# One slot earlier for the second part of batch 0 and the projections of batch 1, in a fused attention and GLU kernel

## The chip, the cores and the metric

The kernel runs on one core of one Trainium2 chip. The metric is the device time of that core in microseconds, as a median over runs. Beside the times there is one profiled execution, whose instructions are told by engine: PE is TensorE (PEld its weight loads), DVE is VectorE, ACT is ScalarE, POOL is GpSimd, SP is SyncE, which issues most of the transfers.

## The reference, cut to what matters

```
# q, k, v: (4 batches, 4 heads, 1088 tokens, 32) float32; S1, S2: (8, 32); x @ w in 128 -> 1536
phi(x) = outer(S1 x, S2 x).reshape(64)            # per token and head
kv, z  = sum_s phi(k_s) v_s^T, sum_s phi(k_s)     # per batch and head
attn   = phi(q) kv / (phi(q) z + 1e-6)
x      = attn transposed to (4352 tokens, 128)
out    = (sigmoid(x @ w_gate) * (x @ w_val)) @ w_out      # d_ff = 1536
```

S1, S2 and the three weight matrices arrive as 64-bit floats. The kernel reads them as pairs of 32-bit words and turns them into 32-bit floats itself.

## The kernel before, in words

The second half, the gated layer, is cut into chunks of 512 tokens (`tok_chk`: eight of 512 and one of 256). A chunk takes twelve **waves**, one for each block of 128 hidden units (the last chunk takes six, of two blocks each). A wave (`w1`, matmuls at line 544) is the gate and the value product of one block; ACT takes the sigmoid (line 552) and DVE multiplies the two (`glu`, line 587). The product with `w_out` follows some waves later: line 425 (`moeout`) in chunk 0, and in chunks 1 to 7 a scheme of seven products of half size (line 381, `prod`) with sums made by POOL (`tsum`, line 371).

Work is issued in **slots** (`slot(group, waves, behind)`). A slot runs its group, then the `glu` of the wave before, then products that have come due, then whatever is given as `behind`, then the next wave. Everything of the attention is placed by hand between slots or as a slot's group. The four compute engines keep the order in which the program issues (`manual_schedule`), each in a queue of its own; a wave is allowed only when its tokens are ready (`moe["ready"]`).

Chunk 0 holds the first 512 tokens of batch 0, whose attention is done ahead of the first wave. During chunk 0 three further things happen:

- The **weights** are converted block by block. Part 0 is gate and value of block 0, part 1 those of block 1, part 2 is `w_out` of blocks 0 and 1, and part n from 3 on is all three matrices of block n-1. The class `Short` does a part in steps: `bounds` (ACT takes the magnitude of the upper words at line 140, POOL limits it at line 141), `lower` (ACT line 152, or DVE line 148, scales the lower words), `shift` (DVE line 157), `total` (POOL line 162, adds), `sign` (ACT line 168) and `final` (DVE line 171, writes `w_sb`). The sign of a part is kept in the PSUM bank `acc1` for parts 2 to 10, and in SBUF for parts 11 and 12. `narrow_w` places these steps in the waves of chunk 0; `final` of part n+1 is normally issued in the wave after the one that issues its `total`.
- The **rest of batch 0**: ACT writes the projected queries `cq` to DRAM (`spread`, line 845), SP reads them back repeated into `qp` and `bq` (line 852), DVE multiplies the two (`qmult(0, 1)`, line 880), PE makes the denominators (`dps`, line 1071, in the bank `acc1`) and the numerators (`nps`, line 1090), and DVE divides in `divide` (transpose, reciprocal, transpose, product into `xT`, lines 1082 to 1111). `part01` does all but the last product, `last01` the product, which makes tokens ready up to 1088 and so allows chunk 1.
- **Batch 1**: `load_kq(1)` loads k and q into the buffer that `bq` of batch 0 used, so SP can issue it only behind `qmult(0, 1)`. Then `turn_k`, `turn_q` (DVE transposes), `begin(1)` (PE projections `kps` and `cqps`, the copy `cq` and its `spread`, which for a whole batch is one write and fourteen reads), two `outer` (DVE), two `sum_z` (DVE), `kv_all` (PE), `qmult(1, 0)`, `weights_z`, `ndt`, `qmult(1, 1)` and `parts(1)` (PE `denj` at line 1029, `nps` at line 1265, then the division).

The waves are counted from 0. Before the change `part01` stands in the slot of wave 10, `last01` in that of wave 11, `begin(1)` in that of wave 13, the two `outer` ahead of the slots of waves 14 and 15, `kv_all(1)` in that of wave 18, `ndt(1)` in that of wave 19, and `parts(1)` in that of wave 22. Batches 2 and 3 are placed by a table of wave numbers (`plan`).

Of the kernel before, what the change touches and what calls it, by code (L numbers as in the profile page):

```python
# [20 lines left out]
def kernel(  # L21
# [19 lines left out]
    NJ = DFF // P  # L41
# [178 lines left out]
    def step(name, *parts, **how):  # L220
        for n in parts if wide else ():
            if n not in short:

                i = ((slice(0, 2), 0), (slice(0, 2), 1), (2, slice(0, 2)))[n] if n < 3 else (slice(0, 3), n - 1)
                pair, jj = (0, i[1]) if n < 3 else divmod(n - 1, 2)
                short[n] = Short(w_sb[:, i[0], i[1]], w_in[pair][:, i[0], jj])
            getattr(short[n], name)(**how)
# [301 lines left out]
    def w1():  # L529

        ci = moe["ci"]
        t0, tw = tok_chk[ci]
        jn = TCH // tw
        j0 = moe["w"] * jn
        wv = psm.tile([P, 2, TCH], F32, tag="wave", name="wave")

        tp = tw // 2 if ci == 0 and j0 == 0 else tw
        turn = (moe["w"] // 2) % 2
        for o in range(0, tw, tp):
            for which in range(2):  # L540
                for jj in range(jn):
                    for c in (0,) if ci == 0 else (1 - turn, turn):
                        d = slice(0, P) if ci == 0 else slice(64 * c, 64 * c + 64)
                        nc.tensor.matmul(  # L544
                            out=wv[d, which, jj * tw + o : jj * tw + o + tp],
                            lhsT=w_sb[:, which, j0 + jj, d],
                            rhs=xT[:, t0 + o : t0 + o + tp],
                            start=True,
                            stop=True,
                        )  # L550
        sg = sbG.tile([P, TCH], F32, tag="sg", name="sg")
        nc.scalar.activation(out=sg, in_=wv[:, 0], func=ACTF.Sigmoid)  # L552
        if ci == 0:
            if j0 == 0:
                step("final", 2)
                step("sign", 3, bank="acc1")
            if j0 == 1:
                step("final", 3)
            if 1 < j0 < NJ - 2:
                narrow_w(j0 + 1, 3)  # L560
            if j0 > 0:
                narrow_w(j0 + 2, 1)
                narrow_w(j0 + 2, 2)
            if j0 < 3:
                narrow_w(j0 + 3, 0)
            if j0 > 1:
                narrow_w(j0 + 4, 0)
            if j0 == NJ - 3:
                weight_sums(0, NJ // 4)
            if j0 == NJ - 1:  # L570
                weight_sums(NJ // 4, NJ // 2)
        if moe["w"] % 2 == 0:
            moe["g"] = sbG.tile([P, 2, TCH], F32, tag="g", name="g")
        pair, odd, n = moe["g"], moe["w"] % 2, moe["n"]

        def glu():
            g = pair[:, odd]
            todo = moe["todo"]
            if jn == 2:
                nc.vector.tensor_tensor(  # L580
                    out=g.rearrange("p (j u s y) -> p j y u s", j=2, u=2, y=4),
                    in0=wv[:, 1].rearrange("p (j y u s) -> p j y u s", j=2, u=2, y=4),
                    in1=sg.rearrange("p (j y u s) -> p j y u s", j=2, u=2, y=4),
                    op=MUL,
                )
            else:
                nc.vector.tensor_tensor(out=g, in0=wv[:, 1], in1=sg, op=MUL)  # L587
            if not fast(ci):
                lag = 4 if ci else 2
                part = (ci, j0, jn, g.rearrange("p (j t) -> p j t", j=jn))  # L590
                todo.append((n + lag, lambda: (w2_end if ci else w2)(*part)))
                return
            if not odd:
                moe["t"] = raw.tile([P, 4, HALF], F32, tag="w_in", name="tsum")
            token_sums(pair, moe["t"], odd)
            if odd:
                part = (ci, j0 // 2, pair, moe["t"])
                todo.append((n + 3, lambda: w2_a(*part)))
                todo.append((n + 4, lambda: w2_b(*part)))

        moe["gate"] = glu
        moe["w"] += 1
        moe["n"] += 1
        if j0 + jn == NJ:
            moe["ci"] += 1
            moe["w"] = 0
# [271 lines left out]
    def qmult(b, n):  # L878
        q0 = half(QP[b], n)
        nc.vector.tensor_tensor(out=q0, in0=q0, in1=half(BQ[b], n), op=MUL)  # L880
# [184 lines left out]
    def dn(b, n, mid=None):  # L1065
        t0, tn = q_chk[n]
        w = 32 * tn
        bank = (moe["sum"] + 1) % 2 if moe["sum"] >= 0 else 1
        dps = pso.tile([P, TCH], F32, tag=f"acc{bank}", name="dps")
        for h in range(H):  # L1070
            nc.tensor.matmul(
                out=dps[32 * h : 32 * h + 32, :w],
                lhsT=zb[:, h, :],
                rhs=half(QP[b], n)[:, 2 * (h % 2) + h // 2, :],
                start=True,
                stop=True,
            )
        dT = sbA.tile([P, 9, 32], F32, tag="dT", name="dT", bufs=1)
        rc = sbA.tile([P, 9, 2], F32, tag="rc", name="rc")

        def turn():
            nc.vector.transpose(out=dT[:, :tn].rearrange("p t c -> p (t c)"), in_=dps[:, :w])

        if mid is not None:
            mid(turn, rc, dT)
        t = ps2.tile([P, 2, 512], F32, tag="two", name="nps")
        for h in range(H):
            for c in range(2):
                rows = slice(64 * c, 64 * c + 64)
                nc.tensor.matmul(  # L1090
                    out=t[32 * h : 32 * h + 32, c, :w],
                    lhsT=ND[b][rows, 32 * h : 32 * h + 32],
                    rhs=half(QP[b], n)[rows, 2 * (h % 2) + h // 2, :],
                    start=True,
                    stop=True,
                )

        def divide(*parts, first=None, between=None, later=False):  # L1100
            if mid is None:
                turn()
                nc.vector.tensor_scalar_add(rc[:, :tn], dT[:, :tn, :2], 1e-6)
            if first is not None:
                first()
            nc.vector.reciprocal(out=rc[:, :tn], in_=rc[:, :tn])
            rb = sbA.tile([P, 9, 2, 32], F32, tag="rb", name="rb")

            def product(u0, u1):
                o = b * S + 64 * (t0 + u0)  # L1110
                nc.vector.tensor_tensor(
                    out=xT[:, o : o + 64 * (u1 - u0)].rearrange("p (t c s) -> p c t s", c=2, s=32),
                    in0=t[:, :, 32 * u0 : 32 * u1].rearrange("p c (t s) -> p c t s", s=32),
                    in1=rb[:, u0:u1].rearrange("p t c s -> p c t s"),
                    op=MUL,
                )
                moe["ready"] = max(moe["ready"], b * S + 64 * (t0 + u1))

            for u0, u1 in parts or [(0, tn)]:
                r0 = rc[:, u0:u1]  # L1120
                nc.vector.transpose(
                    out=rb[:, u0:u1].rearrange("p t c s -> p (t c s)"),
                    in_=bass.AP(
                        tensor=r0.tensor,
                        offset=r0.offset,
                        ap=[list(r0.ap[0]), [1, 2 * (u1 - u0)], [0, 32]],
                    ),
                )
                if between is not None and u0 == 0:
                    between()  # L1130
                if later and u1 == tn:
                    return lambda: product(u0, u1)
                product(u0, u1)

        return divide
# [86 lines left out]
    divide = dn(0, 0, rest)  # L1222
    cq = {}

    def head1():
        turn_q(0, 1)
        step("final", 0)
        step("sign", 1, bank="acc0")
        step("bounds", 2, 3)
        cq[0] = qcomp(0, (1,), (psm, "wave"))  # L1230
        step("lower", 2)

    divide((0, 4), (4, 8), between=head1)
    step("final", 1)
# [13 lines left out]

    late = []

    def part01(first):
        glu()
        late.append(dn(0, 1)(first=first, later=True))

    def last01():
        glu()
# [50 lines left out]
    def kv_all(b):  # L1307
        kv(b, ZS[b])
        kvd(b)
# [2 lines left out]
    spread(0, (1,), cq[0], nc.scalar, nc.sync)  # L1312
    slot(None, 3)
    masks()
    slot(None, 3)
    qmult(0, 1)
    load_kq(1)
    slot(None, 1)
    slot(lambda: part01(lambda: narrow_w(NJ - 1, 3)), 1)
    slot(last01, 1)  # L1320
    load_v(1)
    turn_k(1)
# [9 lines left out]
        slot(None, 1)  # L1332
    slot(lambda: kv_all(1), 1)
    load_v(2)
    qmult(1, 0)
    weights_z(1)
    slot(lambda: ndt(1), 1)
# [71 lines left out]
```

## Time and profile before

| | |
|---|---|
| median of 3 runs | 292.24 us (291.15 to 292.9) |
| the profiled execution's own time | 292.06 us |
| its span, first to last instruction | 290.3 us |
| PE busy | 284.4 us (98%) |
| DVE busy | 171.1 us (59%) |
| POOL busy | 158.7 us (55%) |
| ACT busy | 106.8 us (37%) |
| granted TensorE clock | 1.00 |
| DMA | 24.22 MB, 83 GB/s mean |

A line of the timeline gives the start in us from the span's start, the duration in us, the engine, the source line, the operation, what it writes and reads, and the number of instructions merged; in brackets stands the idle time of the engine before it and what ended that. A matmul in 32-bit floats stands as two records. In chunk 0 a wave is four records of 0.43 us each and the product with `w_out` two more, so a slot takes 2.58 us of PE. Overlapped ends of matmuls make PE look busy even where it starts nothing, so for PE the distances between starts count.

### The profile page before, as it was taken

The numbers are of one execution on the slowest core, as the hardware profiler recorded it, in microseconds if no ns is written. First come the engines' busy times: TensorE is split into PE (matmuls) and PEld (weight loads), VectorE is DVE, ScalarE is ACT, GpSimd is POOL, SyncE is SP. The second block draws the span as 40 slices with busy tenths as digits, with TensorE's granted clock in tenths as the row PEclk, the third lists the DMA queues.
The fourth block names the chain that finished last, engine by engine and source line by source line (L and its number), as shares of the span: only waits on it lengthen the run. The fifth ranks groups of instructions, "written<-read, shape, count | busy, mean of one in ns | idle before, by whom it ended". The sixth has DMA issues, their size and how long they took to land.

```text
span 290.3 us, 5785 instructions
## 1 busy us (share of the span) xinstructions
PE 284.4 (98%) x2262; PEld 152.2 (52%) x2262; DVE 171.1 (59%) x294; ACT 106.8 (37%) x215; POOL 158.7 (55%) x222
## 2 busy tenths in 40 slices
PE   8899999999999999999999999999999999999995
PEld 3444443454444444544554445774555555555895
DVE  6977778965838547666556484737435223522471
ACT  3689832322334222533235222523234223422341
POOL 2466673594356477464455596663465655556200
PEclk9999999999999999999999999999999999999999
DMA  7994440574810385416000863010000100020011
GB/s 215 335 357 101 140 155 0 142 173 99 241 27 2 77 185 140 127 18 174 0 1 9 202 174 68 0 27 12 0 3 9 28 2 0 0 38 1 0 19 38
DMA packets 28890, 24.22 MB, mean 83 GB/s; under 512 B 18560, under 2 KB 24064, under 8 KB 28864
## 3 DMA queue, kind: packets, MB, share of 16 engines
q1 hardware_dynamic: 25808, 21.95, 29.6%
q10 hardware_dynamic: 3056, 1.92, 2.3%
q8 instruction: 17, 0.28, 0.4%
q14 instruction: 9, 0.07, 0.1%
HBM read 20.60 MB, written 3.26 MB: 82 GB/s over the span
## 4 chain that ended last, share of the span: by engine, by line
PE 88%; DMA 7%; DVE 1%; SPq 1%; ACT 1%; issue 1%; POOL 0%; DVEq 0%
PE wave L544 56%; PE prod L381 20%; DMA bq<-dq 5%; PE moeout L425 4%; PE moeout L451 2%; PE nps L1265 1%; DMA a<-dq 1%; PE kps L681 1%; DMA s_in<-in_S_dram 1%; SPq L852 1%; PE kvz L900 1%; DMA dq<-cq 1%; PE cqps L827 1%; PE nps L1090 0%; PE nps L1042 0%
## 5 line engine op out<-in xcount | busy, mean ns | idle before, releaser
L544 PE MATMUL wave<-xT,w_sb 128*64 128x512 f32 (+3 forms) x820 | 210.1, 565 | 0.1
L552 ACT ACTIVATE sg<-wave 128x512 f32<-128x512 f32 x102 | 60.9, 597 | 158.9 <-PE wave L544 152.2
L587 DVE TENSOR_TENSOR g<-wave,sg 128x512 f32<-128x512 f32 x96 | 66.1, 688 | 89.4 <-ACT sg L552 87.1
L544 PEld LDWEIGHTS wave<-xT,w_sb 128*64 128x64 f32 (+1 forms) x820 | 84.2, 140 | 65.6 <-issue 48.8
L371 POOL TENSOR_TENSOR tsum<-g,tsum 128x256 f32<-128x256 f32 x84 | 69.1, 823 | 63.7 <-DVE g L587 63.4
L371 POOL TENSOR_TENSOR tsum<-g 128x256 f32<-128x256 f32 x84 | 65.7, 783 | 31.1 <-DVE g L587 30.6
L381 PE MATMUL prod<-tsum,ws 128*64 128x256 f32 x252 | 70.5, 380 | 0.0
L381 PE MATMUL prod<-g,w_sb 128*64 128x256 f32 x168 | 50.2, 380 | 0.0
L381 PEld LDWEIGHTS prod<-tsum,ws 128*64 128x64 f32 x252 | 32.9, 137 | 10.3 <-issue 7.3
L381 PEld LDWEIGHTS prod<-g,w_sb 128*64 128x64 f32 x168 | 22.7, 137 | 24.7 <-issue 20.8
L381 PE MATMUL prod<-tsum,w_sb 128*64 128x256 f32 x84 | 25.2, 381 | 0.0
L381 PE MATMUL prod<-g,ws 128*64 128x256 f32 x84 | 25.0, 379 | 0.0
L162 POOL TENSOR_TENSOR head<-head,tail 128x384 int32<-128x384 int32 (+1 forms) x13 | 13.1, 1017 | 5.6 <-DVE head L157 4.8
L381 PEld LDWEIGHTS prod<-g,ws 128*64 128x64 f32 x84 | 11.5, 137 | 4.1
L425 PE MATMUL moeout<-g,w_sb 128*128 128x512 f32 (+1 forms) x28 | 12.5, 603 | 0.0
L880 DVE TENSOR_TENSOR qp<-qp,bq 128x1152 f32<-128x1152 f32 (+1 forms) x7 | 10.1, 1436 | 2.9 <-DMA a<-dq 1.8
L381 PEld LDWEIGHTS prod<-tsum,w_sb 128*64 128x64 f32 x84 | 10.5, 136 | 1.8 <-issue 1.0
L760 DVE TENSOR_TENSOR kp<-kab 128x1152 f32<-128x1152 f32 (+2 forms) x10 | 10.8, 1094 | 0.0
L580 DVE TENSOR_TENSOR g<-wave,sg 128x512 f32<-128x512 f32 x6 | 6.6, 1108 | 6.4 <-ACT sg L552 6.4
L141 POOL TENSOR_SCALAR head<-cap 128x384 f32<-128x384 f32 (+1 forms) x13 | 6.2, 482 | 5.6 <-ACT cap L140 5.6
L493 DVE TENSOR_TENSOR res<-prod,other 128x256 f32<-128x256 f32 x14 | 5.9, 423 | 4.7 <-ACT other L484 3.5
L425 PEld LDWEIGHTS moeout<-g,w_sb 128*128 128x128 f32 (+1 forms) x28 | 4.1, 174 | 6.5 <-issue 3.2
(130 smaller groups left out, 199.1 us busy)
## 6 DMA issues: line engine op xcount, KB each, us to landing
qp<-dq SPq DMA_DIRECT2D x7, 576.0 KB
bq<-dq SPq DMA_DIRECT2D x14, 288.0 KB
kq<-in_k_dram SPq DMA_DIRECT2D x3, 544.0 KB
kq<-in_q_dram SPq DMA_DIRECT2D x3, 544.0 KB
w_in<-in_moe_w_out_dram SPq DMA_DIRECT2D x6, 256.0 KB
w_in<-in_moe_w_gate_dram SPq DMA_DIRECT2D x5, 256.0 KB
w_in<-in_moe_w_val_dram SPq DMA_DIRECT2D x5, 256.0 KB
v<-in_v_dram SPq DMA_DIRECT2D x8, 144.0 KB
```

The lines of the kernel that those rows point to most:

```text
L141: nc.gpsimd.tensor_scalar(out=self.head.bitcast(F32), in0=self.cap, scalar1=122880.0, scalar2=2.0**-15, op0=ALU.min, op1=ALU.max,)
L162: nc.gpsimd.tensor_tensor(out=self.head, in0=self.head, in1=self.tail.bitcast(I32), op=ALU.add)
L371: nc.gpsimd.tensor_tensor(out=t[:, u], in0=in0, in1=in1, op=ALU.subtract)
L381: nc.tensor.matmul(out=out, lhsT=lhsT, rhs=rhs, start=start, stop=stop, skip_group_check=True)
L425: nc.tensor.matmul(out=moe["acc"][d], lhsT=w_sb[:, 2, j, d], rhs=g[:, jj], start=(j == 0), stop=(j == NJ - 1),)
L493: nc.vector.tensor_tensor(out=out, in0=in0, in1=in1, op=ALU.add)
L544: nc.tensor.matmul(out=wv[d, which, jj * tw + o : jj * tw + o + tp], lhsT=w_sb[:, which, j0 + jj, d], rhs=xT[:, t0 + o : t0 + o + tp], sta ...
L552: nc.scalar.activation(out=sg, in_=wv[:, 0], func=ACTF.Sigmoid)
L580: nc.vector.tensor_tensor(out=g.rearrange("p (j u s y) -> p j y u s", j=2, u=2, y=4), in0=wv[:, 1].rearrange("p (j y u s) -> p j y u s", j ...
L587: nc.vector.tensor_tensor(out=g, in0=wv[:, 1], in1=sg, op=MUL)
L760: eng.tensor_tensor(out=KP[b][:, pi, j0:j1].rearrange("p j m (i l) -> p (j m) i l", i=R), in0=bass.AP(tensor=a0.tensor, offset=a0.offset, ...
L880: nc.vector.tensor_tensor(out=q0, in0=q0, in1=half(BQ[b], n), op=MUL)
```

## The change

- `part01` moves from the slot of wave 10 to that of wave 9, `last01` from 11 to 10, and all of batch 1 up to `kv_all(1)` and `load_v(2)` moves with them: `qmult(0, 1)` and `load_kq(1)` come behind wave 7 in place of wave 8, and `begin(1)` comes into the slot of wave 12.
- Behind `load_v(2)` one slot without other work is put in, so that `qmult(1, 0)` and all that follows keeps its slot.
- The last `final` of the weights, part 12, was issued inside `divide` of `part01`, ahead of the reciprocal; now `narrow_w` issues it in wave 10 as it does the others. In the same way the `final` of part 11 now stands behind `part01`.
- In the first weights, `lower(2)` on ACT comes ahead of `bounds(3)` and of the copy `cq`; it came behind both.

```diff
@@ w1
-            if 1 < j0 < NJ - 2:
+            if 1 < j0 < NJ - 1:
                 narrow_w(j0 + 1, 3)
@@ divide
-        def divide(*parts, first=None, between=None, later=False):
+        def divide(*parts, between=None, later=False):
...
-            if first is not None:
-                first()
             nc.vector.reciprocal(out=rc[:, :tn], in_=rc[:, :tn])
@@ head1
-        step("bounds", 2, 3)
+        step("bounds", 2)
+        step("lower", 2)
+        step("bounds", 3)
         cq[0] = qcomp(0, (1,), (psm, "wave"))
-        step("lower", 2)
@@
-    def part01(first):
+    def part01():
         glu()
-        late.append(dn(0, 1)(first=first, later=True))
+        late.append(dn(0, 1)(later=True))
@@
     masks()
-    slot(None, 3)
+    slot(None, 2)
     qmult(0, 1)
     load_kq(1)
     slot(None, 1)
-    slot(lambda: part01(lambda: narrow_w(NJ - 1, 3)), 1)
+    slot(part01, 1)
     slot(last01, 1)
@@
     slot(lambda: kv_all(1), 1)
     load_v(2)
+    slot(None, 1)
     qmult(1, 0)
```

The instructions of every engine are the same in kind and number.

## The prediction

> **What bounds the kernel.** I read the page's busy times first, then PE's timeline by the distances between starts, then the other engines where PE's distances are longer than the work.
>
> ```profile
> PE 284.4 (98%) x2262; PEld 152.2 (52%) x2262; DVE 171.1 (59%) x294; ACT 106.8 (37%) x215; POOL 158.7 (55%) x222
> ```
>
> PE bounds. From 19.56 us to the end of chunk 0 its starts stand 0.43 us apart without a hole: one slot is 2.58 us (six records). So an edit can gain only at a hole in PE's starts, and it loses what it opens as a new hole. The timeline of before has two holes that the edit touches. The first is at the start:
>
> ```profile
> 14.90 0.56 ACT L140 ACTIVATE cap<-w_in 128x384 f32<-128x384 f32 x1 [0.53 <-issue]
> 16.14 0.54 ACT L152 ACTIVATE tail<-w_in,two__157 128x256 f32<-128x256 uint32 x1
> 16.77 1.68 POOL L162 TENSOR_TENSOR head<-head,tail 128x256 int32<-128x256 int32 x2 [0.72 <-ACT tail L152]
> 17.52 0.43 DVE L171 TENSOR_TENSOR w_sb<-square,head 128x256 f32<-128x256 f32 x1 [0.60 <-POOL head L162]
> 18.60 0.30 PEld L425 LDWEIGHTS moeout<-g,w_sb 128*128 128x128 f32 x2 [0.86 <-DVE g L587]
> ```
>
> A chain of lower words of part 2 (ACT), total (POOL), final (DVE), `g` (DVE, 17.86 to 18.54) ends at the first product with `w_out`. The last wave record ahead of it starts at 17.98, so PE could have started at 18.40: 0.19 us lost, and the restart costs 0.10 more (the next start is 0.53 us on, not 0.43). The second is in batch 1:
>
> ```profile
> 71.17 1.69 DVE L880 TENSOR_TENSOR qp<-qp,bq 128x1152 f32<-128x1152 f32 x1 [1.77 <-DMA a<-dq]
> ...
> 72.70 0.65 PE L1029 MATMUL denj<-b,zw 64*32 64x160 f32 x16
> 73.52 1.16 PE L1265 MATMUL nps<-qp,nd 64*32 64x512 f32 x32 [0.17 <-DVE g L587]
> ...
> 132.53 0.50 PE L1029 MATMUL denj<-b,zw 64*32 64x160 f32 x16
> 132.82 1.16 PE L1265 MATMUL nps<-qp,nd 64*32 64x512 f32 x32
> ```
>
> From `denj` to `nps` it is 0.82 us in batch 1 and 0.29 in batch 2: 0.53 us lost, since DVE stood waiting for transfers ahead of `qmult(1, 1)` and reached the `g` that `nps` needs late.
>
> What matters most is a place that is no hole yet:
>
> ```profile
> 33.54 0.60 DVE L157 TENSOR_SCALAR head<-head 128x384 int32<-128x384 int32 x1
> 35.04 0.69 DVE L587 TENSOR_TENSOR g<-wave,sg 128x512 f32<-128x512 f32 x1 [0.91 <-ACT sg L552]
> 35.65 0.55 DVE L171 TENSOR_TENSOR w_sb<-square,head 128x384 f32<-128x384 f32 x1
> ...
> 36.63 1.34 DVE L880 TENSOR_TENSOR qp<-qp,bq 128x1152 f32<-128x1152 f32 x1
> 37.89 0.68 DVE L587 TENSOR_TENSOR g<-wave,sg 128x512 f32<-128x512 f32 x1
> ```
>
> ```profile
> 37.59 1.88 PE L544 MATMUL wave<-xT,w_sb 128*128 128x512 f32 x4
> 39.40 0.69 PE L1071 MATMUL dps<-qp,zb 128*32 128x288 f32 x8
> ```
>
> ```profile
> 26.98 0.64 SPq L852 DMA_DIRECT2D qp<-dq  x1
> 27.72 1.27 SPq L852 DMA_DIRECT2D bq<-dq  x2
> 38.00 0.35 SPq L245 DMA_DIRECT2D kq<-in_k_dram  x1
> ```
>
> `qmult(0, 1)` at 36.63 waits for nothing. But its input is fresh. In 26 to 38 us cut into 40 slices of 0.3 us, the transfers' share is
>
> ```profile
> DMA  0000000096999962345546535444300000000000
> GB/s 22 15 0 0 0 0 0 15 292 261 353 323 307 292 138 77 108 154 169 169 169 184 135 108 184 123 108 138 123 15 15 0 0 0 0 0 0 0 0 0
> ```
>
> The last packets of `bq` end at 35.27, and the trace's landing record of its second half is full at 36.00. The multiply had 0.6 us to spare. The change asks for it a slot earlier.
>
> [...]at 71.17 DVE waited 1.77 us and the `g` behind it came after. [...]here the sixteen counts of the write `dq` came between 24.21 and 26.97, and SP issued `qp` at 26.98. [...]sorted by time, each count of `dq` comes 0.13 to 0.40 us behind one of the last `v` load, issued before it. [...]the total that ran beside `qmult` took 2.03 us, its neighbours 1.0.
>
> **The change part by part.**
>
> *Lower words of part 2 earlier.* ACT is idle from 14.37 to 14.90, where it waits for part 3's load. The moved operation takes 0.45 us when followed by another (16.145 to 16.59), so it ends about 14.8 and delays nothing. Then total(2) can start behind the shift, at 16.2 in place of 16.77, and takes 0.72; final(2) follows DVE's `lower(3)`, which ends at 16.92, so it starts at 16.95, and `g` 0.34 later at 17.29, ending 17.97. PE is ready at 18.40. Gain 0.19 + 0.10 = 0.30 us. If the load came earlier than in this execution, ACT would do the magnitude of part 3 up to 0.45 later; that path has slack (part 3's final ends at 19.17, its wave starts 19.56), so the ends are 0 and 0.30; I take 0.30.
>
> *`part01` a slot earlier.* DVE's queue becomes: shift (33.54 to 34.14), `qmult(0, 1)`, `g` of wave 7, final(10), shift, `g` of wave 8, transpose of `dps`. DVE reaches the multiply at about 34.0 and must wait for the landing. SP's reads depend on `dq` alone, which I expect to land as before, so L = 36.00. Response to a landing was 0.12 us at 71.17 (record 71.05). Multiply to the next `g` 1.26 (36.63 to 37.89), `g` to final 0.61, final 0.55, then 0.06 to PE (`g` end 18.54 to 18.60): L + 2.60 = 38.60. Why final(10): `dps` takes bank `acc1`, which holds the sign of part 10 until its final has read it. Before, the same final was done at 36.20, over 3 us ahead of `dps`. PE in turn: wave 8 starts at 35.01 - 0.30 = 34.71, is issued by 36.43, and `dps` would follow at 36.52. So PE stands 2.08 us. Queued behind `dps` on PE are `nps`, the product of wave 7 and wave 9: all wait.
>
> At `dps`, PE still has one product and one wave more to do than before (2.58 us), so the kernel ends later by 38.60 + 2.58 - 39.40 = 1.78 us, the start's gain already in it.
>
> *What follows it.* `load_kq(1)` is released by the multiply, 37.4 in place of 38.0, and its k, landed at 41.92, then lands at 41.4; `turn_k` stands behind final(12) at about 44.5: covered by 3 us. Final(11) now follows the rb transpose, at about 41.7; wave 10 starts at 43.4: covered. Final(12) ends at 44.6, wave 11 starts at 46.0: covered. `begin(1)`: `kps` at 48.8 against turned q at 47.7. The z sums end at about 59.2, `kvz` can start at 60.1: 0.9 us of cover, the thinnest.
>
> *The empty slot.* No instruction of its own. `cq` is copied about 0.8 us earlier than before (PE reaches `cqps` 1.78 - 2.58 = -0.8), so the batch's fifteen transfers start 0.8 earlier while `qmult(1, 1)` comes 1.78 later by DVE's order. Its data, complete at 71.05, come at 70.2; DVE arrives at 71.1. The wait of 1.77 goes, and with it the hole: gain 0.53 (bounds 0.3, if `denj` keeps its own 0.65, to 0.53). The wait of 1.1 us at `qmult(1, 0)` goes too and was worth nothing, since PE had no hole there.
>
> *Sum.* -0.30 + 2.08 - 0.53 = +1.25 us. Against the profiled execution's 292.06 (span 290.3 and 1.8 around it) that is 293.3. The median of the runs lies 0.18 above that execution: 293.5, which is +0.43%.
>
> The whole stands on L: the change is L - 34.75, down to -0.83 where L is below 33.92.
>
> **Rivals.**
>
> *Not slower: the data land earlier.* ACT works up to 0.5 us earlier after the start, so `dq` may be issued before 22.03, and in other executions the slowest of sixteen engines may be less slow (the second slowest count of `dq` was 26.16, 0.8 earlier). For: the multiply's margin hangs on that one engine. Against: the counts follow the `v` load, which does not move. It decides at L = 34.75; with L 0.8 to 2.1 us earlier, 291.4 to 292.7.
>
> *Slower still.* L is later, or a second wait opens: `kvz` loses its 0.9 us of cover when POOL and DVE press each other, or ACT's `dq` slips. Each us of L costs one: L = 37.0 gives 294.5; with a further 0.4 at `kvz`, 294.9. For: the slowest engine sets L. Against: nothing in the change delays `dq`.
>
> *It doesn't do what it says.* Both gains are 0 (the load of part 3 sets the start, `denj` stays slow) and the stall is there: +2.08, 294.3.
>
> *Faster by over 0.5%* needs 1.46 us; both holes hold 0.83. Only something unseen gives it.
>
> **Chances.** The forecast (L between 35.7 and 36.5, 293.2 to 294.0) 0.56; earlier landing 0.20; later landing or second wait 0.13; gains absent 0.07; faster 0.04. A measurement of this kernel can tell about 0.5% from no change: 290.78 and 293.70. Of the forecast's share I put 0.26 above 293.70 and 0.30 below; with the two slower rivals 0.46 slower, with the earlier landing 0.50 the same. The range 291.9 to 294.9 leaves out the faster case, the lower part of the earlier landing and the tail of the later. The likeliest case's own range is 293.2 to 294.0.
>
> **What would show it.** Right: DVE's `qmult` of batch 0 near 36.1 with about 2 us idle before it, released by a transfer of `bq`; `dps` near 38.6, with PE's start before it over 2 us earlier; the first `moeout` at 18.40; `denj` to `nps` 0.3 us in batch 1 and no wait of DVE before its second multiply. Wrong: the multiply at 34 to 35 with little idle time (landing moved), `dps` at 36.5, or a new hole at `kvz` or at waves 10 to 12.

## The result, and the profile after

Six executions of the changed kernel took 295.15 us in the median (294.34 to 296.75), those of the kernel before beside them 292.18. The ratio is 1.0107 with a 95% interval of 1.0074 to 1.014: slower by 2.97 us. In a second measurement (E5 below) seven more executions took 294.4 against 291.68, a ratio of 1.0085 (1.0051 to 1.0118). Forecast were +1.25 us and 293.5, with a range up to 294.9. The sign was right, the size was less than half, and the time lies outside the range.

The profiled execution of after took 294.34 us, 2.28 more than that of before; its span is 292.5 against 290.3. The fences that follow answer to those of the prediction, with the same columns. First the busy times, from the page:

```profile
PE 283.3 (97%) x2262; PEld 151.4 (52%) x2262; DVE 170.2 (58%) x294; ACT 106.6 (36%) x215; POOL 157.9 (54%) x222
```

PE still bounds. The start, from the timelines of ACT, POOL, DVE and PE:

```profile
14.18 0.53 ACT L152 ACTIVATE tail<-w_in,two__157 128x256 f32<-128x256 uint32 x1
14.61 0.56 ACT L140 ACTIVATE cap<-w_in 128x384 f32<-128x384 f32 x1
16.13 1.73 POOL L162 TENSOR_TENSOR head<-head,tail 128x256 int32<-128x256 int32 x2 [0.38 <-DVE head L157]
16.93 0.43 DVE L171 TENSOR_TENSOR w_sb<-square,head 128x256 f32<-128x256 f32 x1 [0.16 <-POOL head L162]
18.31 1.02 PE L425 MATMUL moeout<-g,w_sb 128*128 128x512 f32 x2
```

The lower words of part 2 start at 14.18, the total moves from 16.77 to 16.13, part 2's final from 17.52 to 16.93, and PE reaches the first expert column without a hole. Then the place on which the forecast stood, from the timelines of SP, DVE and PE:

```profile
26.50 0.64 SPq L852 DMA_DIRECT2D qp<-dq  x1
27.23 1.28 SPq L852 DMA_DIRECT2D bq<-dq  x2
...
36.02 1.36 DVE L880 TENSOR_TENSOR qp<-qp,bq 128x1152 f32<-128x1152 f32 x1 [2.21 <-DMA bq<-dq]
37.30 0.68 DVE L587 TENSOR_TENSOR g<-wave,sg 128x512 f32<-128x512 f32 x1
37.90 0.55 DVE L171 TENSOR_TENSOR w_sb<-square,head 128x384 f32<-128x384 f32 x1
...
34.62 1.88 PE L544 MATMUL wave<-xT,w_sb 128*128 128x512 f32 x4
38.50 0.69 PE L1071 MATMUL dps<-qp,zb 128*32 128x288 f32 x8 [2.00 <-DVE w_sb L171]
```

DVE stands 2.21 us before the multiply, released by the transfer of the bias; `g` and final(10) follow it as the prediction had them, and `dps` starts at 38.50 (forecast: 38.60) after 2.00 us of idle PE. And batch 1, from DVE's and PE's timelines:

```profile
70.99 1.35 DVE L880 TENSOR_TENSOR qp<-qp,bq 128x1152 f32<-128x1152 f32 x1
...
74.38 0.50 PE L1029 MATMUL denj<-b,zw 64*32 64x160 f32 x16
74.67 1.16 PE L1264 MATMUL nps<-qp,nd 64*32 64x512 f32 x32
```

DVE waits for nothing before its second multiply, and from `denj` to `nps` it is 0.29 us. No other hole opened: from batch 1's numerators to the end all of PE's starts lie 1.16 us later than before's. The last matmul starts at 287.91 against 286.75: **+1.16 us on PE**, where the sum said +1.25.

So in this execution the mechanism was as forecast, and another 1.1 us came behind the last matmul. The timeline of the last microseconds, first of before, then of after:

```profile
286.92 0.64 ACTq L409 DMA_DIRECT2D out_dram<-o_end  x1
287.38 0.64 SPq L409 DMA_DIRECT2D out_dram<-o_end  x1
```

```profile
288.08 0.64 ACTq L409 DMA_DIRECT2D out_dram<-o_end  x1
288.54 0.64 SPq L409 DMA_DIRECT2D out_dram<-o_end  x1
```

In before the last output packet ends at 289.03, 2.11 us behind the first issue; in after at 291.14, 3.06 behind it. The packet records show what lay between: an instruction fetch of 16 KB stands from 289.25 to 290.43, 270 of the 288 output packets end by 290.18, and the other 18, a sixteenth, run one behind the other from 290.41 to 291.14. From these times I take it that the 18 stood behind the fetch on one of the 16 engines; the records used here do not name the engine. The DMA view from 289 to 291.3 us (queue, packets, MB, share of the 16 engines' time) has that one fetch among the stores:

```profile
q10 hardware_dynamic: 144, 0.07, 10.8%
q1 hardware_dynamic: 144, 0.07, 10.1%
q8 instruction: 1, 0.02, 3.2%
```

That explains 294.34 but not a median of 295.15, and the question for the runs was what takes the other 0.8 us, and whether the tail belongs to the program.

### The profile page after: what moved, and what is told of

The parts are those of the page before. It is cut to its first block, busy times and chain, and to the rows that moved or that the text cites. A ratio compares the mean times of both kernels' runs of the same rounds, so it can differ in the third digit from the quotient of the medians.

```text
span 292.5 us, 5785 instructions
## 1 busy us (share of the span) xinstructions
PE 283.3 (97%) x2262; PEld 151.4 (52%) x2262; DVE 170.2 (58%) x294; ACT 106.6 (36%) x215; POOL 157.9 (54%) x222
## 4 chain that ended last, share of the span: by engine, by line
PE 90%; DMA 5%; DVE 1%; issue 1%; ACT 1%; SPq 0%; DVEq 0%; ACTq 0%
PE wave L544 59%; PE prod L381 21%; DMA bq<-dq 3%; PE moeout L425 2%; PE moeout L451 2%; DMA w_in<-in_moe_w_gate_dram 1%; PE kvz L900 1%; DMA kq<-in_k_dram 1%; PE nps L1264 1%; PE kps L681 1%; PE cqps L827 0%; PE nps L1090 0%; DVE g L587 0%; PE dps L1071 0%; PE denj L1029 0%
## 5 line engine op out<-in xcount | busy, mean ns | idle before, releaser
L162 POOL TENSOR_TENSOR head<-head,tail 128x384 int32<-128x384 int32 (+1 forms) x13 | 12.2, 942 | 9.0 <-DVE head L157 9.0
L880 DVE TENSOR_TENSOR qp<-qp,bq 128x1152 f32<-128x1152 f32 (+1 forms) x7 | 9.5, 1351 | 2.2 <-DMA bq<-dq 2.2
```

What stands on the lines that cost most here:

```text
L162: nc.gpsimd.tensor_tensor(out=self.head, in0=self.head, in1=self.tail.bitcast(I32), op=ALU.add)
```

## The experiments

Runs listed together shared a chip and its executions of before. E1 to E4 stand against 291.74 us (65 executions), E5 to E8 against 291.68 (28), E9 to E11 against 291.92 (28). "First column" is `dps` of batch 0's part 1, "PE's end" the start of the last matmul.

### E1 and E2: each half alone

E1 is before with the edit of `lower(2)`; E2 is after without it:

```diff
-        step("bounds", 2, 3)
+        step("bounds", 2)
+        step("lower", 2)
+        step("bounds", 3)
         cq[0] = qcomp(0, (1,), (psm, "wave"))
-        step("lower", 2)
```

> Before plus the edit of part 2's lower words alone; the slots stay as they were. Theory A (the sum of the prediction holds on TensorE, and the rest of the loss is in the tail): the hole at the first expert column is gone (0.30 us), no wait at the first distance column of batch 0's part 1, last matmul about 286.45 against 286.75. If the tail of before is kept, the time is about 0.3 us under before (291.9 against 292.2); if the 16 KB instruction fetch again falls on the output's transfer, about 0.7 us over it (292.9). Rival B (the lower words themselves cost something later that the profile of after hides): TensorE ends no earlier than in before.

> The shift of the slots alone: part 2's lower words stay behind part 3's magnitudes. Theory A: the wait of the first distance column of batch 0's part 1 for the bias of the keys stands as in after (about 2.1 us; nothing of it depends on the lower words), the hole in batch 1 between denominators and numerators shrinks from about 0.8 to 0.3, and the hole of 0.3 at the first expert column stays: last matmul about 288.2 to 288.3 against 286.75 before, time about 1.5 us over before (293.7) without a late tail and about 2.5 over it (294.7) with one. Rival B (the shift is harmless and the lower words do the harm): time within 0.5 us of before.

**E1: 291.77 us**, ratio 0.9998 (0.9981 to 1.0015), PE's end 286.93. The edit costs nothing and brings nothing that can be measured; of the two expected times neither came. In its profile PE stood 0.36 us late already ahead of the first expert column, it won 0.28 there, and lost 0.1 again in batch 1, where the wait is for data and not for order (DVE's and PE's timelines). So rival B's sign, no earlier end of PE, came too, but PE was late before the edit could tell:

```profile
71.68 1.36 DVE L880 TENSOR_TENSOR qp<-qp,bq 128x1152 f32<-128x1152 f32 x1 [2.20 <-DMA bq<-dq]
...
73.41 0.48 PE L1029 MATMUL denj<-b,zw 64*32 64x160 f32 x8 [0.16 <-DMA b<-dq]
73.69 1.09 PE L1266 MATMUL nps<-qp,nd 64*32 64x512 f32 x16
```

**E2: 293.38 us**, ratio 1.0056 (1.0039 to 1.0072): the loss comes with the slots. The median is 0.3 us under the 293.7 expected. Its profiled execution took 295.37, and this showed what the first one had hidden. PE's timeline:

```profile
38.59 0.69 PE L1071 MATMUL dps<-qp,zb 128*32 128x288 f32 x8 [1.98 <-DVE w_sb L171]
39.22 1.03 PE L1090 MATMUL nps<-qp,nd 64*32 64x288 f32 x16
40.18 2.07 PE L425 MATMUL moeout<-g,w_sb 128*128 128x512 f32 x2
42.05 2.31 PE L544 MATMUL wave<-xT,w_sb 128*128 128x512 f32 x4
```

The same wait as in after (1.98 us), but the matmuls behind it are slow: two expert-column records take 2.07 us where after's took 1.13. The table by stretches, of E2 and then of after's first profile; behind the busy times of PE, weight loads, DVE, ACT and POOL stand the granted clock (1.00 is full speed), the share of the DMA engines and GB/s:

```profile
36.07:39.48 3.41, 1.43 (x18) 0.34 (x24) 3.37 (x6) 1.13 (x3) 0.74 (x2) 1.00 0.26 61
39.48:42.89 3.41, 3.41 (x19) 1.17 (x4) 2.29 (x6) 0.00 (x0) 1.29 (x2) 0.50 0.66 265
```

```profile
34.46:37.88 3.42, 2.04 (x5) 0.57 (x3) 1.86 (x2) 2.61 (x6) 0.94 (x2) 1.00 0.03 9
37.88:41.29 3.41, 2.79 (x28) 1.15 (x29) 3.31 (x9) 0.00 (x0) 1.00 (x1) 1.00 0.83 277
```

In E2 PE's clock was halved for one stretch of 3.41 us behind the wait. Against after's first profile PE stood 0.09 us late at the first column and 1.75 at the end: the halved stretch cost **1.66 us**. A second one begins in E2's records at 292.07, after PE's work; the two starts are 252.59 us apart, 74 times 3.413. The clock records of after and of before start 3.74 and 4.58 us from the span's start, and the clock falls to half at 290.46 and 291.30: 286.72 us on in both, 84 times 3.413. So in these three traces the starts and changes lie whole steps of 3.413 us apart, counted from another moment in each execution, and the stretches here are laid out by that grid. E2's wait lay inside one stretch (36.07 to 39.48, of which PE was busy 1.43: 1.98 us idle), after's was cut by a boundary at 37.88 into 1.38 and 0.62, and nothing was halved there. From here on this was the theory, and the rival was that the wait costs its length only, with all else in the landing of the bias.

### E3, E4 and E10: shorten the wait

E3 loads batch 1's v from ACT's queue where the code has `load_v(1)` (in after SP issues these loads at 18.1 to 20.2, ahead of the wait for `dq`; ACT comes to them at 43.4); E10 does it directly behind `spread(0)`; E4 lets part 10's sign stay in SBUF, so that the first column needn't wait for final(10):

```diff
 E3   -    load_v(1)
      +    load_v(1, nc.scalar)
 E10       spread(0, (1,), cq[0], nc.scalar, nc.sync)
      +    load_v(1, nc.scalar)
           ...
      -    load_v(1)
 E4   -            step("sign", j + 1, bank="acc1" if j < NJ - 2 else None)
      +            step("sign", j + 1, bank="acc1" if j < NJ - 3 else None)
```

> After, but batch 1's v is loaded from ScalarE's queue, issued behind its last work of the stage, so that the bias that the queries' product needs is no longer queued behind v's 16 packets. Theory A (the bias lands late because its packets stand behind v's on each DMA engine): the bias lands about 2 us earlier than its 35.9, the first distance column waits under 0.3 us, last matmul 1.5 to 2.1 us earlier than in after (286 against 287.9); time 1.3 to 2 us under after. If v is then late, batch 1's projection of v waits for it, which would show at that matmul. Rival B (the bias has its own latency of some 14 us from issue, whatever is in front of it): it lands at 35 to 36 as in after and the time is that of after.

> After, but the sign of weight part 10 goes to SBUF as those of the later parts do, not to the bank acc1 of PSUM that the first distance column writes. Theory A (the column waits 0.12 + 1.26 us for VectorE's product with the bias, and then another 1.2 us for the final words of part 10 and the square of the heads only because part 10's sign sits in its bank): the column starts at the end of the product, about 37.4 instead of 38.5, and the last matmul is about 1.0 to 1.1 us earlier than in after. Rival B (the bank is not what gates; part 10's final words or a later operation of VectorE gate the next matmul anyway): the column starts earlier but the next matmul waits for what it waited for, and the last matmul moves by under 0.3 us.

> After, but batch 1's v is loaded from ScalarE's queue directly behind the write of the changed layout, so that this write no longer stands behind v on the DMA engines, and v comes early enough for batch 1's projection of v. Theory A (the bias lands late because its whole chain starts where the initial loads end, with v the last of them, at 26.0): the write lands at about 24, the bias 2 us earlier than in after, at about 34, the first distance column waits under 0.3 us, no wait at batch 1's projection of v; with the hole at the start and that of batch 1 gone too, last matmul at about 286.0 against 286.75 before, time 0.5 to 0.8 us under before (290.9 to 291.2), with no execution of clock 0.995 or less. Rival B (ScalarE's four issues, 0.44 us each, delay the sigmoids and TensorE behind them; or the queries' transfers now share the engines with v and land no earlier): time over before.

**E3: 292.38 us** (1.0025, 1.0013 to 1.0037). With v out of the way `qp` is issued at 23.97 in place of 26.50, 2.39 us behind the issue of `dq`, and the multiply finds its data:

```profile
23.97 0.65 SPq L852 DMA_DIRECT2D qp<-dq  x1
...
33.80 1.35 DVE L880 TENSOR_TENSOR qp<-qp,bq 128x1152 f32<-128x1152 f32 x1
...
36.67 0.69 PE L1071 MATMUL dps<-qp,zb 128*32 128x288 f32 x8
...
48.87 1.08 PE L544 MATMUL wave<-xT,w_sb 128*64 128x512 f32 x4 [0.80 <-ACT cq L835]
```

Theory A held at the first column (1.83 us earlier than in after). What it did not foresee is another wait: not for v, but 0.80 us until ACT's copy of `cq` is done. The copy itself is not late: it starts 0.50 us behind the last projection record in E3 and 0.51 in after, and v's loads had been issued from 43.4 to 45.2, 3 us ahead of it. In after the wave at this place starts without waiting for the copy; why it waits in E3 is not shown. PE's end is 286.95, where 286 was expected.

**E4: 292.41 us** (1.0020, 1.0007 to 1.0033). Theory A held: the first column is released by the multiply itself, and PE's end is 286.79, 1.12 us earlier than in after.

```profile
37.38 0.69 PE L1071 MATMUL dps<-qp,zb 128*32 128x288 f32 x8 [0.95 <-DVE qp L880]
```

**E10: 292.21 us** (1.0016, 1.0003 to 1.0028). The write landed as early as in E3 (`qp` issued at 23.98), but the bias only about 1.1 us earlier than in after: the multiply starts at 34.87, after a wait of 1.16 us for `bq`, not at 34. Expected was 290.9 to 291.2; `dps` at 37.34 still waits 0.88 us, PE's end is 286.76, and the time lies over before, as rival B had it. Why `bq` took longer here stays open; v's packets now lie between it and the write.

### E5: the changed kernel again

> The changed kernel itself once more, beside the others of this study. Theory A (TensorE's halved clock): besides the wait of 2.0 us at the first distance column, some executions lose a further 1.3 to 1.7 us because the granted clock is halved for one stretch of 3.41 us behind the wait, as the profile of the shift alone showed from 39.48; those executions show a mean granted clock of 0.990 to 0.995. Median about 293.3 to 294.3, with two groups about 1.5 us apart. Rival B (the late tail of the first profile of after is a property of the program): in this profile again an instruction fetch of 16 KB lies on the output's last packets, and every execution is about 1 us longer than its last matmul says.

**294.4 us**, seven executions from 292.52 to 296.3; three of them have a mean granted clock of 0.993 or 0.994, as four of the first six had 0.990 to 0.994. One stretch at half clock makes 1 - 0.5 x 3.41 / 293 = 0.994. (A halving behind PE's last matmul, as in after's first profile from 290.46 on, costs nothing and took the mean there to 0.996; so only 0.995 and less is counted in what follows.) The three are the three longest of the seven, 294.81 to 296.3. Rival B of the tail fell: here the last output packet ends 2.10 us behind the first issue, as in before, and the instruction fetch came at 293.27, after the end. In the thirteen other profiles of this study the time is 5.3 to 5.7 us more than PE's end, in after's first 6.4. The late tail is an accident of one execution.

The profiled execution, at full clock, shows a third thing. In it the transfers came late from the start:

```profile
15.78 0.57 ACT L140 ACTIVATE cap<-w_in 128x384 f32<-128x384 f32 x1 [1.13 <-issue]
...
27.40 0.64 SPq L852 DMA_DIRECT2D qp<-dq  x1
...
37.20 1.36 DVE L880 TENSOR_TENSOR qp<-qp,bq 128x1152 f32<-128x1152 f32 x1 [2.31 <-DMA bq<-dq]
...
39.68 0.69 PE L1071 MATMUL dps<-qp,zb 128*32 128x288 f32 x8 [2.10 <-DVE w_sb L171]
```

`qp` is issued 0.90 later than in the first profile, the multiply starts 1.18 later, and PE keeps all of the 1.18 to its end (289.09). Before, the multiply had 0.6 us to spare; after, each late landing is passed on.

### E6 and E9: fill the wait

Matmuls on constants, whose result nothing uses, in front of the first column; E9 has `range(2)` in place of `range(4)`:

```diff
     def part01():
         glu()
+        fill = ps2.tile([P, 2, 512], F32, tag="two", name="fill")
+        for _ in range(4):
+            nc.tensor.matmul(
+                out=fill[:, 0],
+                lhsT=nc.const_aps.tensor(1.0, [P, P], F32),
+                rhs=nc.const_aps.tensor(1.0, [P, 512], F32),
+                start=True,
+                stop=True,
+            )
         late.append(dn(0, 1)(later=True))
```

> After, with four matmuls of 512 columns on constants (0.43 us each, 1.7 us together) put in front of the first distance column of batch 0's part 1, where TensorE waits for 2.0 us anyway. Their result is used by nothing. Theory A (the wait costs more than its length, because an idle TensorE is granted half its clock in the next stretch of 3.41 us): TensorE's work behind the wait stays where it is in the profiles without a halved stretch (last matmul about 287.9), the executions with a mean clock of 0.990 to 0.995 are gone, and the upper group of times with them: median 0.3 to 1 us under that of after, and no execution over 295. Rival B (the wait costs its length only): same times as after, or up to 0.1 us more.

> After, with two matmuls of 512 columns on constants in front of the first distance column of batch 0's part 1; each takes two passes, 1.77 us together by the eight passes of 3.55 us that the four of the run before took, against a wait of 2.0 to 2.1 us. Theory A (an idle TensorE is granted half its clock in the next stretch of 3.41 us): TensorE's idle time at this place falls to 0.2 to 1 us, the executions with a mean clock of 0.990 to 0.995 (3 of 7 for after here, 4 of 6 at first) are gone, and since TensorE's work behind the column is not moved by the filling, the highest time falls from 296.3 to under 294.5 and the median by 0.3 to 1 us, to 293.3 to 294.0. Rival B (the spread of after's times comes from the landing of the bias alone): the median and the highest time stay as they were.

**E6: 294.7 us**, but the filling was mis-sized: each matmul of 512 columns in 32-bit floats stands as two records, so that four took 36.55 to 40.09 and held the first column up themselves (PE's end 289.50). So it can't tell what the wait costs, but its six executions lie between 294.43 and 295.1, all at clock 1.0.

**E9: 293.19 us**, six executions from 292.82 to 293.37, ratio 1.0042 (1.0027 to 1.0057), mean clock 0.999 or 1.0 in all. PE's timeline:

```profile
34.62 1.88 PE L544 MATMUL wave<-xT,w_sb 128*128 128x512 f32 x4
36.34 1.89 PE L1254 MATMUL fill<-const-float32-1.0 128*128 128x512 f32 x4
38.42 0.69 PE L1071 MATMUL dps<-qp,zb 128*32 128x288 f32 x8 [0.20 <-DVE w_sb L171]
```

The first column starts where it did (38.42 against 38.50), PE's end is 287.83 against 287.91: the useful work has not moved. Yet the median is 1.2 us under the 294.4 of E5 and the longest execution 2.9 us under E5's. The intervals of the two ratios still touch (1.0027 to 1.0057, and 1.0051 to 1.0118 in E5); what sets them apart is the clock, low in none of the twelve executions of E6 and E9 and in seven of after's thirteen. Rival B, by which nothing should have changed, falls: beside the wait's length, PE's idleness in it costs time. What remains over before (291.92) is 1.27 us.

### E7 and E11: lengthen the wait

E7 writes the changed layout one slot later; E11 loads v twice:

```diff
 E7   -    slot(None, 2)
      +    slot(None, 3)
           spread(0, (1,), cq[0], nc.scalar, nc.sync)
      -    slot(None, 3)
      +    slot(None, 2)
 E11       load_v(1)
      +    load_v(1)
```

> After, but the change of layout of batch 0's second part one slot later (three slots ahead of it and two behind it), so that the bias of the queries lands one slot, about 1.9 us, later. Theory A: the wait of the first distance column grows from 2.0 to about 3.9 us[...]: TensorE ends 1.9 + 1.3 to 1.7 = 3.2 to 3.6 us later than in after's first profile, less what batch 1's remaining hole of 0.29 can't give back: last matmul 291 to 291.5, mean clock of every execution at or under 0.995, time about 3.3 us over after without a halved stretch (296.5 to 297.5). Rival B (the wait costs its length only): +1.9 us, 295 to 295.5, clock 1.0 in most executions.

> After, with batch 1's v loaded twice (three of the four repeated loads stand ahead of the queries' transfers on SyncE's queue), so that the bias lands later by the time of a transfer and its landing, about 2 us. Theory A (halved clock): the wait of the first distance column grows from 2.0 to about 4 us[...]: mean clock 0.995 or less in all of them, and last matmul later than in after by the added wait and by 1.3 to 1.7 us at least. Rival B (a wait costs its length only): later by the added wait alone, clock 1.0 in most executions.

**E7: 294.49 us**, and the edit did not do what it was made for. `dq` was issued at 23.82 in place of 21.56, but `qp` at 26.33, no later than in after: 2.51 us behind the write's issue, close to E3's 2.39. So between these two moments the issue of `dq` does not set the landing. With E3 this points to what does: the loads of the start, which end near 26.0 with v as the last. As a repeat of after it gave a wait of 2.37 us, and three of six executions with a clock of 0.990 to 0.993. The profiled one had full clock; its stretches at the wait and at the end of the kernel show why:

```profile
34.36:37.78 3.42, 2.12 (x5) 0.57 (x4) 1.41 (x2) 2.69 (x6) 0.94 (x2) 1.00 0.05 12
37.78:41.19 3.41, 2.34 (x27) 0.93 (x28) 3.31 (x8) 0.00 (x0) 1.00 (x1) 1.00 0.70 222
286.95:290.36 3.41, 1.59 (x30) 1.34 (x25) 0.29 (x1) 0.27 (x1) 0.00 (x0) 1.00 0.11 31
290.36:293.78 3.42, 0.00 (x0) 0.00 (x0) 0.00 (x0) 0.00 (x0) 0.00 (x0) 1.00 0.04 12
```

The wait was cut by a boundary into 1.30 and 1.08 us of idle PE, as E5's of 2.10 us was into 0.76 and 1.34. And at the end 1.82 us without PE were still followed by full clock, where in E12's profile 2.09 us at the same place were followed by half. In the 14 profiles of this study, from the first stretch at full clock on and with the ends of matmuls as the profiles model them, every stretch with 1.98 us or more of idle PE is followed by a halved one, and none with 1.82 or less. So in these profiles not the length of a wait alone decides, but how much of it falls into one stretch.

**E11: 295.91 us.** The second load delayed the bias by 0.7 us, not 2, and the wait is 2.54 us, so what a wait of about 4 us does was not shown. Four executions of six had a low clock (0.992 to 0.994; 295.89 to 296.77), while the two at full clock took 293.23 and 293.57. Neither theory A's "in all of them" nor rival B's "clock 1.0 in most executions" held. The profiled one, by stretches:

```profile
36.89:40.30 3.41, 1.07 (x24) 0.34 (x24) 3.41 (x6) 0.94 (x2) 0.78 (x1) 1.00 0.31 73
40.30:43.71 3.41, 3.41 (x16) 1.51 (x5) 2.10 (x6) 0.00 (x0) 1.30 (x3) 0.50 0.62 254
```

PE was 0.73 us later than in after at the first column and 2.38 later behind the halved stretch: 1.65 us for it, as in E2.

All kernels together, by the idle time of PE ahead of the first column in their profiles:

| kernels | wait, us | executions | with a mean clock of 0.995 or less |
|---|---|---|---|
| after (two measurements), E7 | 2.0 to 2.4 | 19 | 10 |
| E2 | 2.0 | 20 | 3 |
| E11 | 2.5 | 6 | 4 |
| E3, E4, E10 | under 1.0 | 66 | 0 |
| E6, E9 (filled) | 0 to 0.2 | 12 | 0 |
| before, E1, E8 | none | 157 | 2 |

The two of the last row and one of E2's (297.29 us) stand at 0.988, by the sum above two halved stretches; none of the three was profiled.

Of after's thirteen executions the seven with the low clock took 295.50 us in the mean, the other six 293.81: 1.69 apart.

### E8 and E12: the holes that the prediction counted as gains

E8 keeps batch 0's part 1 and batch 1's projections where before has them and takes only `lower(2)` and the empty slot behind `load_v(2)`, so that batch 1 from `qmult(1, 0)` on comes a slot later. Against before:

```diff
-        step("bounds", 2, 3)
+        step("bounds", 2)
+        step("lower", 2)
+        step("bounds", 3)
         cq[0] = qcomp(0, (1,), (psm, "wave"))
-        step("lower", 2)
...
     slot(lambda: kv_all(1), 1)
     load_v(2)
+    slot(None, 1)
     qmult(1, 0)
```

E12 is before once more, unchanged, for a second profile.

> Before with the edit of the lower words, and of the slots only the empty one behind batch 1's kv: batch 0's last part and batch 1's projections stay where they are in before, the part of batch 1 from its first product with the bias on comes one slot later. Theory A (the hole of 0.82 us between batch 1's denominators and numerators is there because VectorE reaches the product with the second bias 1.8 us before its transfers are done; one slot more covers it): the hole shrinks to 0.29, the wait at batch 0's first distance column stays absent, and the gain of 0.30 at the start, which lower words alone lost again at this hole (0.90 us there), is kept: last matmul about 0.8 us earlier than in before (286.0), time 0.5 to 0.8 under before. Rival B (a slot later pushes batch 2's loads and the planned slots behind it so that another wait comes up): no gain or a loss.

> The kernel before once more, for a second profile of it. Theory A (the two holes of before that the prediction counted as gains, 0.30 us at the first expert column and 0.53 of the 0.82 us between batch 1's denominators and numerators, hang on when loads land and so differ from execution to execution; that is why neither the lower words alone nor the later slot alone shortened the median by what the profile promised): at least one of the two differs by over 0.15 us here, and the last matmul lies 0.2 us or more away from 286.75. Rival B (they are fixed by the program): both holes as in the first profile, to 0.1 us.

**E8: 291.51 us**, ratio 1.0004 (0.9988 to 1.0019). Its profile shows all that theory A asked for: no wait at the first column, `denj` to `nps` in 0.29 us, PE's end at 285.78, 0.97 earlier than in before's.

```profile
74.83 0.50 PE L1029 MATMUL denj<-b,zw 64*32 64x160 f32 x16
75.12 1.16 PE L1266 MATMUL nps<-qp,nd 64*32 64x512 f32 x32
```

But the time that it asked for, 0.5 to 0.8 under before, did not come: the median is 0.17 under that of before, which can't be told from nothing; of both kernels the shortest span is 289.2 us. It doesn't beat before; it is 2.9 us quicker than after.

**E12** (one execution, 291.71) divides the two holes. From ACT's and PE's timelines:

```profile
14.51 0.55 ACT L140 ACTIVATE cap<-w_in 128x384 f32<-128x384 f32 x1 [0.32 <-issue]
...
72.33 1.01 PE L1029 MATMUL denj<-b,zw 64*32 64x160 f32 x16
73.16 1.15 PE L1265 MATMUL nps<-qp,nd 64*32 64x512 f32 x32
```

The one in batch 1 is there again, 0.83 us from `denj` to `nps`. The one at the start has shrunk from 0.30 to 0.10 us: ACT waits 0.32 there in place of 0.53. PE's end is 286.39, so theory A held. Of the 0.30 us that the sum credited, 0.20 were not there in this second execution.

## Why the prediction was right or wrong

- **"The whole stands on L"**, and the chain behind it: right to 0.1 us in the first profile. Wait of DVE 2.21 (forecast: about 2), multiply at 36.02, `dps` at 38.50 (38.60), final(10) and its bank as the last gate (E4 takes the bank away: 1.12 us back). That L was hit so closely is partly luck: in the eight profiles with the moved slots and v ahead of `dq` the multiply started between 35.72 and 37.20.
- **"2.08 us" for the stall**: the measured distance from PE's being free to `dps` is 2.0. This is the term that failed. The sum prices idle PE at its length. The runs show that idle PE of this length also risks a stretch of 3.41 us at half clock, at 1.65 to 1.66 us each (E2, E11), in 10 of 19 executions of after and E7, and that no execution had it where the idle time was filled (E6, E9) or under 1.0 us (E3, E4, E10). For after that is, as an estimate, 7/13 x 1.66 = 0.9 us in the mean.
- **"-0.30" and "-0.53"**: both happened in after's profile, and the covers that were named (`turn_k`, final(11) and (12), `kps`, `kvz` at 60.28 with the z sums done at 59.83, half of the 0.9 us forecast) all held. As gains against before's median they are less sure: E1 alone gained nothing, E8 with both 0.17 us, and E12 puts the first at 0.10.
- **The sum of +1.25**: E9, which is after with the wait filled, is 1.27 us over before, by its interval 0.8 to 1.7. So the sum was about right for what it counted, and +1.16 on PE in after's first profile says the same. That the two agree to 0.02 us is luck: by E8 the gains of 0.83 in the sum are hardly there against before's median.
- **"Its span and what lies around it"**: the sum took the tail behind the last matmul as fixed. In after's first profile it was 1.0 us longer, where an instruction fetch of 1.17 us met the last output; in E5, E7 and E9 it wasn't. That is noise of single executions, but it brought the first profile's loss (2.28 us) near the median's (2.97) for a reason of its own.
- **The rivals**: "slower still" gave 294.5 by L = 37.0, "each us of L costs one". E5's profile is that case (multiply at 37.20, 294.4 us), and it is part of the spread, but not what carries the median: E9 makes the same transfers in the same order and lies at 293.19. "The data land earlier" did not occur in any profile with v ahead of `dq`. "The gains absent" gave nearly the first profile's time (294.3) by a mechanism that did not happen.
- **"Each count of `dq` comes 0.13 to 0.40 us behind one of the last `v` load"**: in before's landing records it is 0.17 to 0.40, and in after's as well (v's sixteen counts from 23.45 to 26.08, those of `dq` from 23.80 to 26.48). What the prediction drew from it, that the write lands when v does, held: from the issue of `dq` to that of `qp` it is 4.94 us behind v's loads in after and 2.39 with v away (E3), and where `dq` was issued 2.26 us later with v ahead, `qp` was issued at 26.33, no later than after's 26.50 (E7).

**Left open.** Why E2, with the same wait in its profile, has the low clock in only 3 of 20 executions. If half clock needs between 1.82 and 1.98 us of a wait of 2.0 us in one stretch, and the grid lies anywhere, that is by an estimate (3.41 - 2.0 + 2 x 0.02) / 3.41 = 43% to (3.41 - 2.0 + 2 x 0.18) / 3.41 = 52% of all cases. The 10 of 19 of after and E7 fit that; for E2 8 to 10 of 20 were to be expected. Six of E2's executions took under 293.0 us, less than its wait would leave (291.74 + 2.08 - 0.53 = 293.3), so they may have waited less; no profile shows it. Nor does one show where the low clocks without a wait at this place come from. And after's six executions without a low clock (293.81 in the mean) lie 0.6 us over E9's six (293.16). Two of the six are the profiled ones, with the late tail (1.0) and the late transfers (1.18), which would make 0.36 of it; the rest is open.

## What to carry to other kernels

Price a wait of the bounding engine at its length only where it is short: on TensorE here waits under 1.0 us were followed by no low clock in 66 executions (E3, E4, E10), while those of 2.0 to 2.4 us cost their length and, in 10 of 19 executions of two kernels and 3 of 20 of a third, about 1.7 us more. One profile may not show this, but the mean granted clock of each execution does (0.995 or less), and useless matmuls in the wait, if shorter than it, took it away (0.999 or 1.0 in E9's six executions). Where a step is moved up to fresh data, its cover was also what absorbed late landings (0.6 us before; after, E5's 1.18 us went through to PE's end whole), so ask for their spread and not only for the landing in one profile. And ask which loads are under way ahead of a small transfer: with v's loads ahead, `dq` issued 2.26 us later moved the issue of `qp` by only 0.17 us (E7 against after); with them away it came 2.53 us earlier (E3).

## What the runs showed of the hardware that I had not expected

- PE's clock was halved for one stretch of 3.41 us behind 1.98 and 2.34 us of idle PE within the stretch before (E2, E11), not behind 1.38 (after) or 1.82 (the end of E7's profile); the cost was 1.65 to 1.66 us each time.
- A 16 KB instruction fetch took 1.17 us, and where it met the last output, this ended about 1.0 us later behind its issue than in before (3.06 against 2.11 us, after's first profile); where it came at 293.27 (E5) or 287.32 (E9), it cost nothing.
- A write of 144 KB took 2.4 us from issue to its use with v's loads away, and 4.9 us behind 0.5 MB of loads in another queue (E3 against after); issued 2.26 us later behind the same loads, it took 2.5 (E7).
